# A chunked RWKV layer with a squared-ReLU FFN on one core: state products in four array quarters, a repacked first chunk, and squares on ScalarE

## The chip, the cores and the metric

The kernel runs on one core of one Trainium2 chip. The metric is the time of one execution on the device in microseconds (us); the median of three runs is given. Engines are named as the profile names them: PE is TensorE's matmuls and PEld its weight loads, DVE is VectorE, ACT is ScalarE, POOL is GpSimd, and SP and ACTq are the two queues from which DMAs are issued.

## The reference

For each of 4 batches and 8 heads a state of 48 x 48 runs over 768 tokens; the result, laid out as 3072 tokens x 384, goes through a dense FFN of width 2048 whose activation is the square of a ReLU.

```python
for t in range(S):                                   # S = 768, D = 48
    cur = einsum('bhd,bhe->bhde', u * k[t], v[t])
    y[t] = einsum('bhd,bhde->bhe', r[t], state + cur)
    state = w[t][..., None] * state + einsum('bhd,bhe->bhde', k[t], v[t])
x = y.transpose(0, 2, 1, 3).reshape(B * S, H * D)    # 3072 x 384
h = maximum(x @ w_in, 0.0)                           # 384 x 2048
out = (h * h) @ w_out                                # 2048 x 384
```

## The kernel before

The 768 tokens are cut into six chunks (`c`) of 128. Chunk and batch make a *unit* of attention, 24 in all. The eight heads of a unit lie as four pairs `p`; of a pair, head `j = 0` stands on partitions 0 to 47 and head `j = 1` on partitions 64 to 111, so a pair fills 112 rows. In a unit, w is multiplied up along the tokens by scans (L478), its reciprocal comes from `Ln` and `Exp`, r and k are scaled by both, and then come four kinds of products on PE. `scores` (step `mt`, L526) makes the 128 x 128 score matrices of the heads; DVE puts them under the causal mask into tiles whose diagonal ACT has set (`diag`, L515) from `beta`, the sum over a head of -r k u. `inter` (L552) multiplies the incoming state `Ss[b]` by r and `part` (L560) multiplies values by masked scores; both add into one PSUM bank `yb`, and together they are the step `mix` of the chunks after the first. `outer` (step `dS`, L611) makes the new state. ACT and DVE then split y into two fp32r halves (step `x`, L591 and L592). Chunk 0 has no incoming state.

For chunk 0, r, k and w are loaded with the tokens on the partitions, 192 bytes to a packet, into tiles `st0`; PE transposes them into PSUM (step `turn`, L466). Later chunks are turned by DVE block transposes and DMAs instead. In all chunks `beta` comes from two POOL multiplications (L505, L507) and a DVE sum (L508).

The FFN has 16 slices `f` of width 128. For each, nine products (three rows of 128 inputs, each as three fp32r products) fill a PSUM bank `hp` with 512 tokens, or 256 in half steps (L640); ACT takes the ReLU (L645), DVE squares it (L646), ACT rounds it to fp32r (L648) and DVE takes the rest (L649). Then three products for each batch add to `ob` (L655), which stays in PSUM for the whole chunk. The weights are loaded in eight groups in the first 100 us and split into two fp32r parts by ACT, DVE and POOL in turn (L383 to L404).

All of it is written as steps, each with an engine, a cost, a rank and the tiles that it reads and writes. The class `Plan` plays the steps through with these costs; at each point the step that can start first on its engine goes next, and among equals that of the lower rank. The result is one fixed order of instructions per engine. The ranks are the numbers of the class `Ranks`. Tiles are drawn from pools: there are two PSUM banks `a` for all attention products, two `hp`, and two tiles `q` for split weights and for results on their way out. Where `Plan` sees PE idle in the first 110 us, it inserts *fillers*, transposes of the identity whose result nobody reads (L681). After the plan a flag is made from `far`, which tells whether any w lies outside the range that this way of computing can bear; every engine reads it, and a slow path that follows is skipped.

## Time and profile before

| | us |
|---|---|
| median of 3 runs (lowest, highest) | 550.34 (550.27, 550.54) |
| the profiled execution's own time | 549.26 |
| its span from the first to the last instruction | 547.30 |
| PE busy in the span, fillers among it | 532.6 |
| fillers (L681), 97 in banks `a` and 33 in banks `hp` | 19.5 |
| DVE, ACT, POOL busy | 357.1, 287.3, 102.3 |

The profiled execution is 1.08 us under the median. Its clock for TensorE was granted at 0.996 over the span. Rows of the timeline give the start, the length, the engine, the line of the source, the operation and the number of instructions merged into the row, and in brackets how long the engine had been idle and on whom it had waited. Rows of windows give, for each stretch of time, the busy time of each engine and its instructions. An fp32 matmul of the attention appears in the trace as two instructions (passes); one of the FFN, in fp32r, as one.

### The profile page before, as it was taken

Reading aid. Unit: us, or ns where it says so; the run is one execution under the profiler, and the core shown is the slowest. Engines: PE = TensorE matmul, PEld = TensorE weight load, DVE = VectorE, ACT = ScalarE, POOL = GpSimd, SP = SyncE. Lnnn points to the kernel's source line nnn. Section 1 sums busy time; section 2 is a strip of 40 time slices with the busy share of each in tenths; the row PEclk is TensorE's granted clock in tenths of the full one; section 3 lists DMA queues with packets and bytes.
Section 4 is the critical chain, followed back from the end, with each engine's and each line's share of the span. In section 5 each row is a group of like instructions: output and inputs, shape, how many; then the busy total and the mean of one; then the engine's idle time right before and its main releaser. Section 6 shows DMA issues by size and latency. Waiting matters only on the chain. (4 is left out here: it accounts for less than half of the span.)

```text
span 547.3 us, 10350 instructions
## 1 busy us (share of the span) xinstructions
PE 532.6 (97%) x3930; PEld 474.5 (87%) x3930; DVE 357.1 (65%) x650; ACT 287.3 (52%) x677; POOL 102.3 (19%) x119
## 2 busy tenths in 40 slices
PE   7899999999999999999999999999999999999995
PEld 6778988889998989888888888888888889899994
DVE  5889989999587775958667747656855332333331
ACT  2886885566855845655643654545553332332322
POOL 5335653540212020210302002003000000000000
PEclk9999999999999999999999999999999999999998
DMA  9999699156563825455553723703411000000001
GB/s 164 216 244 272 128 245 206 24 90 136 115 132 64 169 47 105 97 104 99 101 107 62 138 73 60 142 3 73 74 57 30 1 0 16 29 31 1 0 1 62
DMA packets 206456, 50.88 MB, mean 93 GB/s; under 512 B 196161, under 2 KB 201281, under 8 KB 206401
## 3 DMA queue, kind: packets, MB, share of 16 engines
q1 hardware_dynamic: 205680, 49.17, 44.0%
q10 hardware_dynamic: 720, 0.98, 0.6%
q8 instruction: 33, 0.54, 0.4%
q14 instruction: 23, 0.18, 0.1%
HBM read 31.65 MB, written 4.72 MB: 66 GB/s over the span
## 5 line engine op out<-in xcount | busy, mean ns | idle before, releaser
L655 PE MATMUL ob<-wo,g 128*128 128x384 f32 x1152 | 226.9, 341 | 0.5 <-ACT g L648 0.5
L640 PE MATMUL hp<-x,wi 128*128 128x512 f32 (+1 forms) x1062 | 222.7, 355 | 1.4 <-DVE g L649 0.9
L655 PEld LDWEIGHTS ob<-wo,g 128*128 128x128 f32 x1152 | 199.3, 188 | 9.2 <-ACT g L648 0.7
L640 PEld LDWEIGHTS hp<-x,wi 128*128 128x128 f32 x1062 | 174.5, 188 | 27.5 <-DVE g L649 2.3
L645 ACT ACTIVATE t<-hp 128x512 f32<-128x512 f32 (+1 forms) x118 | 61.1, 518 | 154.2 <-PE hp L640 132.5
L646 DVE SCALAR_TENSOR_TENSOR hp<-hp,t 128x512 f32<-128x512 f32 (+1 forms) x118 | 70.3, 596 | 102.0 <-ACT t L645 101.5
L649 DVE TENSOR_TENSOR g<-hp,g 128x512 fp32r<-128x512 f32 (+1 forms) x118 | 68.9, 585 | 38.1 <-ACT g L648 37.3
L648 ACT CAST g<-hp 128x512 fp32r<-128x512 f32 (+1 forms) x118 | 59.5, 505 | 55.7 <-DVE hp L646 55.6
L515 ACT ACTIVATE m<-ident,beta 128x128 f32<-128x128 f32 x192 | 60.4, 395 | 1.2 <-DVE beta L508 1.2
L505 POOL TENSOR_TENSOR st<-st 128x384 f32<-128x384 f32 x24 | 26.6, 1108 | 61.7 <-DVE st L432 54.5
L620 POOL TENSOR_TENSOR S<-S,Ec 112x192 f32<-112x192 f32 x16 | 8.3, 523 | 142.2 <-DVE S L619 142.2
L530 DVE COPY_PREDICATED m<-caus,a 128x512 f32<-128x512 uint8 x48 | 33.3, 730 | 0.7 <-PE a L526 0.6
L478 DVE TENSOR_TENSOR_SCAN pt<-pt,zero 112x128 f32<-112x128 f32 x80 | 30.3, 426 | 3.0 <-DMA v<-in_v_dram 1.3
L526 PEld LDWEIGHTS a<-pt 48*128 48x128 f32 x384 | 23.6, 187 | 7.3 <-issue 5.1
L526 PE MATMUL a<-pt 48*128 48x128 f32 x384 | 28.3, 285 | 1.1 <-DVE pt L498 1.1
L560 PE MATMUL a<-m,v 128*48 128x128 f32 (+1 forms) x384 | 27.2, 279 | 1.0 <-DVE m L530 1.0
L432 DVE STREAM_TRANSPOSE st<-st 128x1152 f32<-128x1152 f32 x20 | 27.2, 1366 | 0.0
L560 PEld LDWEIGHTS a<-m,v 128*48 128x48 f32 (+1 forms) x384 | 20.0, 128 | 6.4 <-issue 4.6
L592 DVE SCALAR_TENSOR_TENSOR x<-a,x 112x128 fp32r<-112x128 f32 (+2 forms) x44 | 17.5, 431 | 12.3 <-ACT x L591 11.7
L507 POOL TENSOR_TENSOR st<-st,un 128x384 f32<-128x384 f32 x24 | 25.1, 1047 | 1.6
L404 POOL TENSOR_TENSOR wi<-q,wi 128x768 fp32r<-128x768 f32 x8 | 17.6, 2204 | 38.0 <-ACT wi L403 31.5
L495 DVE TENSOR_TENSOR pt<-pt,m 112x512 f32<-112x512 f32 x24 | 17.4, 728 | 8.9 <-ACT m L486 8.3
(78 smaller groups left out, 417.1 us busy)
## 6 DMA issues: line engine op xcount, KB each, us to landing
pt<-st SPq DMA_DIRECT2D x80, 96.0 KB, 2.3
ro<-in_moe_w_out_dram SPq DMA_DIRECT2D x8, 768.0 KB, 7.5
v<-in_v_dram SPq DMA_DIRECT2D x24, 192.0 KB, 3.4
st<-in_w_dram SPq DMA_DIRECT2D x11, 384.0 KB, 4.2
st<-in_k_dram SPq DMA_DIRECT2D x11, 384.0 KB, 5.4
st<-in_r_dram SPq DMA_DIRECT2D x11, 384.0 KB, 5.6
pt<-st SPq DMA_DIRECT2D x80, 48.0 KB, 2.5
out_dram<-q SPq DMA_DIRECT2D x20, 192.0 KB, 1.9
```

The costliest lines, as they stand in the source:

```text
L432: V.transpose(out=zt[:, i].rearrange("a t p q i -> a t (p q) i"), in_=sv[:, :, i].rearrange("s t p q x -> s t (p q) x"))
L478: lambda p=p: V.tensor_tensor_scan(out=pt[:, 0, p], data0=src(0)[:, p], data1=zero.broadcast_to([HP, C]), initial=1.0, op0=ALU.mult, op1=A ...
L515: A.activation(mv(j)[:, p], ident, AF.Copy, scale=beta.tile[:, 2 * p + j:2 * p + j + 1])
L526: T.matmul(mts[j].tile.rearrange("s (p t) -> s p t", p=NP)[:, p], pt[js, 2, p], pt[js, 1, p], start=True, stop=True)
L530: lambda j=j: V.copy_predicated(out=mv(j), mask=caus.unsqueeze(1).broadcast_to([128, NP, C]), data=mts[j].tile.rearrange("s (p t) -> s p t ...
L560: T.matmul(ybv()[to:to + n + D, spot(p)], vt.tile[:, o - n:o + D], mv(j)[:, p], start=(c == 0 and p == SPLIT), stop=True, skip_group_check ...
L640: T.matmul(hp.tile[:, 0:n], wi[f][:, wl, kt], xT[:, kt, xl, xs], start=(m == 0), stop=(m == 3 * KT - 1))
L645: P.add("act", 0.5 if full else 0.28, rank("g"), lambda: A.activation(t(), h(), AF.Relu), r=[hp], w=[(g, 1)])
L646: P.add("dve", 0.61 if full else 0.33, rank("g"), lambda: V.scalar_tensor_tensor(out=h(), in0=h(), scalar=0.0, in1=t(), op0=ALU.max, op1=A ...
L648: P.add("act", 0.53 if full else 0.31, rank("g"), lambda: A.copy(out=hi(), in_=h()), r=[hp], w=[(g, 0)])
L649: P.add("dve", 0.61 if full else 0.33, rank("g"), lambda: V.tensor_tensor(out=lo(), in0=h(), in1=hi().bitcast(F32), op=ALU.subtract), r=[h ...
L655: T.matmul(obs[b][:, 0:DM], g.tile[0][:, gl, o:o + C], wo[f][:, wl], start=(f == 0 and m == 0), stop=(f == NF - 1 and m == 2))
```

## The change

1. *State products in four quarters.* `inter` runs the pairs in the order 0, 3, 2, 1. For pairs 3 and 1 (`ACROSS`) the result of head `j` goes to the other half of the PSUM partitions, and into a second bank `far_yb`, in `inter` and in `part`. So the rows used (0 to 47 or 64 to 111) and the columns used (0 to 63 or 64 to 127) make four combinations. `mix` now needs both banks `a`, and y is split in three parts instead of two (`outs`). One weight load of each group is cut in two so that its rows match the swapped halves.
2. *Chunk 0.* w, k and r of a batch come in one DMA each, whose partitions are head and block of 8 tokens: 128 packets of 1,536 bytes instead of 1,024 of 192. `turn` is now 16 products with columns of the identity per tensor (each two passes) instead of 4 transposes. `beta` is formed after the turn: ACT copies -k, DVE multiplies by r, PE multiplies by `ut`, which holds u as columns, and ACT copies the result. `ut` is made from two small DMAs on ACT's queue into a tile `u8` that DVE clears first, one transpose on PE and two ACT copies. `un`, still used by later chunks, is loaded later from SP's queue.
3. *FFN of chunk 0.* Its 22 steps (12 half, 10 full) are squared by ACT.
4. *The last results* go out through four tiles `m`. Batches 0 and 2 are copied by ACT and stored from ACT's queue, 1 and 3 by DVE and stored from SP's; of batch 3, ACT copies one half.
5. *The flag* is made by steps of the plan, with a 1 x 1 product.
6. `Plan` has a changed rule for who may claim tiles, new constants, and all ranks are new (`Ranks`, of which the diff shows a line).

```diff
-    AT = {'load': -105.75, 'z': 279.5, 'pt': 293.75, ...}
+    AT = {'load': 311.75, 'z': -350, 'pt': -3.75, ...}
-    LANES, RUNS, SLACK, START = 8, 2300, 2.0, 2.4
+    LANES, RUNS, SLACK, START = 8, 2300, 2.0, 1.4
-    IDLE = (110.0, 4.0, 0.3, 0.12)
+    IDLE = (110.0, 2.8, 0.3, 0.12)
...
+    ACROSS = (3, 1)
...
-    nc.scalar.dma_start(out=un, in_=u.rearrange("h d -> (h d)").partition_broadcast(128))
+    u8 = P.pools["m"][1][1][0:H, 0:HP]
+    V.memset(u8, 0.0)
+    for j in range(2):
+        nc.scalar.dma_start(out=u8[:, j * J:j * J + D], in_=u)
+    us = Slot("hp")
+    P.add("pe", 0.1, -300, lambda: T.transpose(out=us.tile[0:HP, 0:H], in_=u8, identity=ident[0:H, 0:H]), w=[us])
...
+            for b0 in (b, b + 1) if c == 0 else ():
+                        nc.sync.dma_start(out=st.tile.rearrange("s (t b x) -> s t b x", t=3, b=2)[:, i, b0 - b, 0:TB * D],
+                                          in_=src[b0, :, ss, :].rearrange("h (a s) d -> h a (s d)", s=TB))
...
-                    for p in range(NP):
-                        T.transpose(out=to[:, p], in_=pairs[:, p], identity=ident)
+                    for y in range(TB):
+                        for j in range(2):
+                            n = (J, D)[j]
+                            T.matmul(to[j * J:j * J + n, :, :, y], rows[:, y * D:y * D + n], pick[:, :, j], start=True, stop=True, ...)
...
+        if c == 0:
+            P.add("act", ..., A.activation(pt[:, 2], src(2), AF.Copy, scale=-1.0), ...)
+            P.add("dve", ..., V.tensor_tensor(out=pt[:, 2], in0=pt[:, 2], in1=src(1), op=ALU.mult), ...)
+            def sums():
+                for p in range(NP):
+                    T.matmul(tl(ps[0])[:, 2 * p:2 * p + 2], pt[:, 2, p], ut[:, p], start=True, stop=True, ...)
...
+        side = lambda p, j: 1 - j if p in ACROSS else j
         def inter():
-            for p in (*TILES, SPLIT):
+            for p in (0, 3, 2, 1):
                 for j in range(2):
-                    T.matmul(ybv()[j * J:j * J + n + D, spot(p)], Ss[b][js, ...], pt[js, 1, p], start=(spot(p) == 0), ...)
+                    T.matmul(spot(p)[to:to + n + D], Ss[b][js, ...], pt[js, 1, p], start=(p in (0, 3)), ...)
...
-        P.add("dve", ..., V.scalar_tensor_tensor(out=h(), in0=h(), scalar=0.0, in1=t(), op0=ALU.max, op1=ALU.mult), ...)
+        if c == 0:
+            P.add("act", ..., A.activation(h(), t(), AF.Square), r=[(g, 1)], w=[hp])
+        else:
+            P.add("dve", ..., V.scalar_tensor_tensor(out=h(), in0=h(), scalar=0.0, in1=t(), op0=ALU.max, op1=ALU.mult), ...)
...
-                os_ = Slot("q")
+                os_ = Slot("m" if end else "q")
...
+    P.add("pe", 0.2, rank, lambda: T.matmul(fps.tile[0:1, 0:1], flag, one, start=True, stop=True), r=["flag"], w=[fps])
```

The start of PE before (`ident` is the identity, `st_135` holds w, k and r of batches 0 and 1, `ob` and `a` are PSUM banks):

```order
L681 MATMUL a_145<-ident 128x128 x19
L466 MATMUL ob_139<-ident,st_135 128x128 x4
L681 MATMUL a_145<-ident 128x128 x2
L466 MATMUL ob_141<-ident,st_135 128x128 x4
L681 MATMUL a_145<-ident 128x128 x2
L466 MATMUL ob_140<-ident,st_135 128x128 x4
```

The start of PE after, with what each row waits for (`m_157` is the tile `u8`; the DMAs named in its first row are the two loads of u; the second row holds fillers):

```order
L359 MATMUL hp_145<-ident,m_157 112x8 [waits DMAHW3_49,DMAHW5_49,DVE_49,Pool_49]
L750 MATMUL a_147<-ident 128x128 x17
L497 MATMUL ob_141<-ident,st_135 64x64 [waits DMAHW0_49]
L497 MATMUL ob_141<-ident,st_135 48x64
```

The transpose of u has come to the head of PE, ahead of the fillers and the first turn; there are 81 fillers in all instead of 130, and behind the first FFN product there are 2 of them instead of 31.

The state and value products of one unit on PE before (`S_129` is the state, `a_145` the one bank):

```order
L552 MATMUL a_145<-pt_127,S_129 64x128
L552 MATMUL a_145<-pt_127,S_129 48x128
L552 MATMUL a_145<-pt_127,S_129 64x128
L552 MATMUL a_145<-pt_127,S_129 48x128
L552 MATMUL a_145<-pt_127,S_129 64x128
L552 MATMUL a_145<-pt_127,S_129 48x128 x3
L560 MATMUL a_145<-m_158,v_151 64x128
```

The same place after, with two banks `a_148` and `a_147`:

```order
L706 MATMUL ob_141<-wo_75,g_97 128x384 x3
L599 MATMUL a_148<-pt_127,S_130 64x128
L599 MATMUL a_148<-pt_127,S_130 48x128
L599 MATMUL a_147<-pt_127,S_130 48x128
L599 MATMUL a_147<-pt_127,S_130 64x128
L599 MATMUL a_148<-pt_127,S_130 64x128
L599 MATMUL a_148<-pt_127,S_130 48x128
L599 MATMUL a_147<-pt_127,S_130 48x128 x2
L607 MATMUL a_148<-m_162,v_153 64x128
```

Eight matmuls stay eight, two for each of the four combinations. Over the whole program PE goes 157 times from one kind of array use to another (full, row halves, column halves, quarters) instead of 133 times.

At the end of DVE's program, after, the flag's comparison (L749), which waits for PE's last product, stands ahead of the two copies of results:

```order
L700 TENSOR_TENSOR g_97<-hp_145,g_97 128x512 [waits PE_49,Activation_49]
L749 TENSOR_SCALAR flag_i<-a_147 1x1 [waits PE_49]
L714 COPY m_159<-ob_142 128x384
L714 COPY m_160<-ob_144 128x192 [waits Activation_49]
L757 TENSOR_LOAD flag_i [waits DVE_49]
```

On SP, too, the reading of the flag stands ahead of the two stores of these copies. Before, no result was copied by DVE there.

More of the change, by code (lines that the diff above doesn't have):

```diff
@@ L198 @@
-    LAG = 2
+    AT = {'load': 311.75, 'z': -350, 'pt': -3.75, 'rk': -45.75, 'beta': 190.5, 'far': 301, 'v': 372.5, 'scan': -67.25, 'ln': -130.75, 'rt': -69.25, 'kn': -35, 'diag': 45.75, 'mt': -197.75, 'mask': 253.5, 'ktp': -331.25, 'kt': -191.75, 'mix': -146.25, 'x': -182.25, 'x3': -366.5, 'send': -58.75, 'dS': -74, 'S': -10.25}
+    AT0 = {'load': -134, 'turn': -192.5, 'rk': -234, 'beta': -426.75, 'far': 167.25, 'v': -18.75, 'scan': -53, 'ln': -344.75, 'rt': -84.5, 'kn': -137, 'diag': -76.75, 'mt': -424.25, 'mask': -23, 'ktp': 40.5, 'kt': 228.75, 'mix': -2.75, 'x': -429.5, 'x3': -190.5, 'send': -251, 'dS': -102.25, 'S': 256}
@@ new lines @@
+    AT1 = {'load': 67, 'z': 273.25, 'pt': 29, 'rk': 446, 'beta': 16.75, 'far': -195.5, 'v': 267.25, 'scan': 136, 'ln': -57.25, 'rt': 198.5, 'kn': 72.75, 'diag': 386.5, 'mt': -559.25, 'mask': 9.5, 'ktp': -539.5, 'kt': 139, 'mix': -229.25, 'x': 106.25, 'x3': -193.5, 'send': -227.75, 'dS': -127.75, 'S': -232.5}
+    U0 = (-253.75, -214.25, -115, 73.5)
+    C1 = (-20.75, -24.5, 124.5, 44.25)
+    W0 = (-174, -102.5, -39.75, 50.5, 165.75, 85.5, 71.25, 211.75)
+    WL = (-14, -12.25, 110, 5, 3, -5.25, -285, 23.5)
@@ L200, in unit @@
+    OFF = {'hp': 1, 'g': -172, 'ob': 6.25, 'os': -416.25}
+    LAG = -0.5
     def unit(self, c, b, name):
@@ L680, with bad @@
             x += step
+    flag, one, flag_i = (const.tile([128, 1], t, name=n) for n, t in (("flag", F32), ("one", F32), ("flag_i", I32)))
+    G.memset(one, 1.0)
+    fps = Slot("a")
+    rank = RANKS.unit(NC - 1, B - 1, "far") + 1
+    def bad():
+        V.tensor_reduce(out=flag, in_=far, axis=AX.X, op=ALU.max)
+        V.tensor_scalar(out=flag, in0=flag, scalar1=0.0, scalar2=None, op0=ALU.is_gt)
+    P.add("dve", 0.2, rank, bad, r=[("far", c, b) for c in range(NC) for b in range(B)], w=["flag"])
+    P.add("pe", 0.2, rank, lambda: T.matmul(fps.tile[0:1, 0:1], flag, one, start=True, stop=True), r=["flag"], w=[fps])
+    P.add("dve", 0.1, rank, lambda: V.tensor_scalar(out=flag_i[0:1], in0=fps.tile[0:1, 0:1], scalar1=0.0, scalar2=None, op0=ALU.is_gt), r=[fps], w=["flag_i"])
     P.filler = lambda bank: T.transpose(out=bank[:, 0:128], in_=ident, identity=ident)
```

172 lines of the change are left out of this document (98 added, 74 removed).

## The prediction, made before the changed kernel was timed

> **What bounds the kernel.** I read the page first, then the windows by stage, then the timeline of the start, of one unit of attention, and of the end. The page says that PE is busy almost throughout:
>
> ```profile
> PE 532.6 (97%) x3930; PEld 474.5 (87%) x3930; DVE 357.1 (65%) x650; ACT 287.3 (52%) x677; POOL 102.3 (19%) x119
> ```
>
> That share holds fillers, so I took it apart by stage: first up to the first FFN product (34.71), then to the last filler, then the long middle, and what follows PE's last FFN product. The first five rows are all instructions, with PE, PEld, DVE, ACT and POOL in turn, the last two the fillers alone.
>
> ```profile
> 0.00:34.71 34.71, 29.36 (x272) 24.71 (x272) 26.70 (x61) 21.14 (x54) 17.22 (x33) 1.00 1.06 207
> 34.71:80.00 45.29, 43.15 (x357) 38.66 (x358) 41.06 (x73) 36.70 (x87) 22.06 (x13) 1.00 0.91 213
> 80.00:300.00 220.00, 219.39 (x1772) 197.13 (x1771) 171.84 (x321) 129.96 (x325) 51.13 (x58) 1.00 0.54 105
> 300.00:540.55 240.55, 240.55 (x1534) 213.92 (x1532) 117.34 (x196) 98.52 (x212) 11.87 (x16) 1.00 0.20 42
> 540.55:547.30 6.75, 0.12 (x3) 0.03 (x1) 0.16 (x1) 0.96 (x2) 0.00 (x0) 0.65 0.35 118
> ...
> 0.00:34.71 34.71, 15.34 (x99) 12.90 (x99) 1.00 1.06 207
> 34.71:80.00 45.29, 4.20 (x31) 3.58 (x31) 1.00 0.91 213
> ```
>
> From 80 to 540.55 PE idles 0.61 us: there every microsecond of PE work counts in full. Ahead of 34.71 PE does 29.36 - 15.34 = 14.0 us of real work; 20.7 are filler or idle. From there to 80 another 4.20 + 2.14 = 6.3 are. With the 0.61 that makes 27.6 us of empty time, and the tail is 6.75. So three things can move the end: PE's work, the empty time in the first 80 us, and the tail.
>
> What makes the early time empty is DVE, and ahead of it the first turn:
>
> ```profile
> 1.05 1.50 DVE L307 MEMSET st<- 128x768 f32 x2 [1.05 <-PEq L770]
> 1.61 4.32 PE L681 MATMUL a<-ident 128*128 128x128 f32 x19 [1.61 <-POOL ident masks.py:199]
> 2.56 0.59 DVE L343 MEMSET v<- 128x128 f32 x4
> 6.08 0.89 PE L466 MATMUL ob<-ident,st 128*128 128x128 f32 x4
> 7.01 1.37 DVE L478 TENSOR_TENSOR_SCAN pt<-ob,zero 112x128 f32<-112x128 f32 x4 [2.81 <-PE ob L466]
> 12.21 4.31 PE L681 MATMUL a<-ident 128*128 128x128 f32 x38
> ...
> 7.00:34.71 27.71, 23.65 (x46) 1.00 1.15 226
> 34.71:99.00 64.29, 58.05 (x97) 1.00 0.89 203
> ```
>
> The last two rows are DVE alone: from its first scan it works 23.65 of the 27.71 us to the first FFN product, and 58.05 of 64.29 after that. The filler rows also give PE's pace: 128 columns in 4.32 / 19 = 0.227 us at the start, although the windows show a granted clock of 1.00, and 4.31 / 38 = 0.113 later.
>
> **Quarters.** One unit:
>
> ```profile
> 98.89 1.08 PE L552 MATMUL a<-pt,S 48*64 48x128 f32 x16
> 99.91 1.09 PE L560 MATMUL a<-m,v 128*64 128x128 f32 x16
> 103.57 0.67 PE L611 MATMUL a<-v,m 128*64 128x48 f32 x16
> 104.16 2.37 PE L655 MATMUL ob<-wo,g 128*128 128x384 f32 x12
> ```
>
> The 16 passes of `inter` take 99.91 - 98.89 = 1.02 us. At 0.113 a pass singly they would take 1.81, in pairs 8 x 0.113 = 0.90; so two run at once, and 0.12 goes for the change of array use. Four at once need 4 x 0.113 = 0.45: 0.45 less a unit, 20 units, **-9.0 us**. Bounds: 0 if quarters do not overlap further, -9.0 if they do fully. L560 uses all 128 rows for every pass and also gets 16 passes into 1.02 us, so two column halves already share rows; and L611's 16 passes take 104.16 - 103.57 - 0.12 = 0.47, that is 0.029 each with their weight loads, and four of those fit into 0.12. I take the full end.
>
> [...]
>
> **Added PE work.** `turn`: 32 passes of 64 columns with weights as in L611. 0.029 each if the weight loads set the pace (0.94), 0.039 if columns do (1.25); L611 has the same weights, so 1.0, against 4 x 0.113 = 0.45: 12 x 0.55 = +6.6 (5.9 to 9.6). `sums`: 8 passes with 128 columns of weights and 2 that stream, between 8 x 0.029 = 0.23 and a filler's 8 x 0.113 = 0.90; its weight load is a filler's, so four times 0.90, +3.6 (0.9 to 3.6). Changes of array use: 24 more at about 0.11, +2.6. PE's work: -9.0 + 6.6 + 3.6 + 2.6 = **+3.8**.
>
> **What I cost at nothing.** y is split in three parts, one ACT and one DVE instruction more in each of 20 units:
>
> ```profile
> L591 ACT ACTIVATE x<-a 112x128 fp32r<-112x128 f32 x20 | 5.4, 269 | 1.1 <-PE a L560 1.1
> L592 DVE SCALAR_TENSOR_TENSOR x<-a,x 112x128 fp32r<-112x128 f32 x20 | 5.6, 282 | 3.5 <-ACT x L591 3.5
> ```
>
> Both engines have room behind 80 us (129.96 and 171.84 of 220); uncovered, 0.55 a unit would make 11 us. `mix` now waits for both banks `a`, and FFN products are queued behind it on PE; `scores` has always taken both banks, and PE still idled only 0.61 us. The eight extra DMA issues for weights, the later load of `un`, and the loads of batches 2 and 3, which SP now issues ahead of the first weights, are covered by DVE's 27 us of work ahead of the first FFN product; at 207 GB/s the first 2.8 MB take 13.5 us. If that cover went, a weight group would be late by one DMA's landing, about 5 us. POOL only loses work.
>
> **The empty time.** First the new wait. PE's first instruction needs u, which needs DVE's clearing of `u8`. DVE starts at 1.05; two small clearings, `ut`, the four of L343 (0.59) and the rest put `u8` near 2.1. Then ACT issues two DMAs. Prices for issue and landing:
>
> ```profile
> 540.50 0.34 ACTq L662 DMA_DIRECT2D out_dram<-q  x1
> ...
> x<-x SPq DMA_DIRECT2D x60, 32.0 KB, 2.0
> ...
> un<-in_u_dram ACTq DMA_DIRECT2D x1, 192.0 KB, 4.5
> ```
>
> The second is issued near 2.45 and lands between 4.5 and 7.0; being small, I take 4.9. Behind it, in order on PE, stand 17 fillers at the slow pace, 3.9, then the first turn, 1.0: the first scan starts near 9.8 instead of 7.01. Larger packets help here only if the fillers are not in the way, and they are.
>
> From the first scan to the first FFN product DVE now has 52 instructions instead of 46: four products and two masks more, four instructions of a weight split, one block transpose; three reductions and two state updates fewer.
>
> ```profile
> L432 DVE STREAM_TRANSPOSE st<-st 128x1152 f32<-128x1152 f32 x20 | 27.2, 1366 | 0.0
> L498 DVE TENSOR_TENSOR pt<-pt,m 112x512 f32<-112x512 f32 x20 | 13.7, 684 | 0.2
> L530 DVE COPY_PREDICATED m<-caus,a 128x512 f32<-128x512 uint8 x48 | 33.3, 730 | 0.7 <-PE a L526 0.6
> L508 DVE TENSOR_REDUCE beta<-st 128x8 f32<-128x384 f32 x24 | 12.9, 539 | 0.9 <-POOL st L507 0.9
> L396 DVE SCALAR_TENSOR_TENSOR q<-ro,q 128x768 uint32<-128x768 uint32 x8 | 8.7, 1082 | 0.0
> L619 DVE TENSOR_TENSOR S<-a,S 112x192 f32<-112x192 f32 x16 | 5.6, 352 | 4.3 <-PE a L611 4.1
> ```
>
> 4 x 0.68 + 2 x 0.73 + 4 x 0.9 + 1.37 - 3 x 0.54 - 2 x 0.35 = +6.8; durations overlap a little, so +6. That gives 29.7, and 2.6 of waits (4.1 before): the first FFN product at 42.1. PE's own count agrees: real work 14.0 + 7.1 (twelve turns for eleven) + 2.7 (three `sums`) + 1.1 (one more `mt`) = 24.9, plus 4.9, 3.9, 62 fillers at 0.113 = 7.0 and 1.4 of waits. So 17.3 us are empty there. But now three units and two weight groups are ready instead of two and one.
>
> Behind it, DVE loses the 22 squares:
>
> ```profile
> L646 DVE SCALAR_TENSOR_TENSOR hp<-hp,t 128x512 f32<-128x512 f32 x74 | 51.5, 697 | 95.0 <-ACT t L645 94.9
> L646 DVE SCALAR_TENSOR_TENSOR hp<-hp,t 128x256 f32<-128x256 f32 x44 | 18.8, 426 | 7.0 <-ACT t L645 6.6
> ```
>
> 12 x 0.43 + 10 x 0.70 = 12.1 us less where DVE had 6.2 to spare. ACT takes them at about L645's price (0.38 and 0.60): 10.6 more on some 49 of 64 us. So I leave 1.7 of the 6.9 us of later emptiness, 0.2 of it fillers. Empty time: 19.0 against 27.6, **-8.6** (-5 to -12).
>
> **The tail.**
>
> ```profile
> 540.71 0.16 DVE L696 TENSOR_SCALAR flag_i<-a 128x1 int32<-128x1 f32 x1 [3.71 <-PE a L694]
> 541.47 0.48 ACT L660 COPY q<-ob 128x384 f32<-128x384 f32 x1 [1.00 <-DMA out_dram<-q]
> 542.41 0.48 ACT L660 COPY q<-ob 128x384 f32<-128x384 f32 x1 [0.47 <-SPq L698]
> 542.92 1.02 ACTq L662 DMA_DIRECT2D out_dram<-q  x1
> ```
>
> Copies no longer wait for two buffers. But the flag's comparison, which ends at 540.87, now stands ahead of DVE's two copies, and SP reads the flag ahead of its stores: the last store is issued near 542, not 542.92. **-1.0** (0 to -2).
>
> **Sum.** +3.8 - 8.6 - 1.0 = -5.8. The profiled execution took 549.26, which becomes 543.5; the median of the runs lies 1.08 above, so **544.5 us**.
>
> **Rivals.** (a) *Slower:* quarters that share rows do not overlap. The term of 9.0 falls away, and the added turns and sums stay: 553.5. It decides from the point where less than 3.2 of the 9.0 are had. For it speaks that no row shows more than two passes at once; against it L560 and L611. 10%. (b) Half of the overlap, with weight loads of the four in each other's way: 549.0. 9%. (c) u lands early or the fillers do not delay the first turn, and the scan starts at 7 after all: 541.7. Large packets speak for it, the order of PE against. 15%. (d) ACT becomes what DVE was: the squares wait behind `diag` and weight splits, and the 5.2 us that I took out behind the first FFN product come back: 549.7. ACT's 49 + 10.6 of 64 us speak for it. 14%. (e) Writing the turned tensors in steps of 32 bytes doubles a turn; twelve more microseconds, half of them in empty time: 550.5. No row shows such writes. 7%.
>
> **Numbers.** The forecast has 45%. Measurements of this kernel tell a change from none at about 0.2%, 1.1 us: 549.2 to 551.4 is no change. Faster: the forecast, (c), and about two thirds of (b) and (d), 0.78; the same 0.10; slower, (a) and the upper ends of (d) and (e), 0.12. The range 539.5 to 550.5 leaves out (a) and some of (c) and (e).
>
> **What would show it.** Right: a quarter row of 16 passes with some 0.57 us to the next row; the first scan near 9.8; the first FFN product near 42 and hardly a filler after it; the last store near 542. Wrong: 1.0 us for the quarters, PE waiting on ACT's square between 45 and 130 us, or, since both banks `a` go to one `mix`, new idle time of PE before products into `a` behind 130.

## The result, and the profile after

| | us |
|---|---|
| changed kernel, median of 8 runs (lowest, highest) | 547.41 (546.44, 549.32) |
| kernel before, median of 8 runs on the same chip | 550.54 (549.46, 551.28) |
| ratio, 95% interval | 0.9946 (0.9931 to 0.9961) |
| the profiled execution's own time, its span | 547.43, 545.6 |

The change makes the kernel faster by 3.1 us; 5.8 were forecast. The direction was right, and the size is about half. In the pair of profiled executions the span went from 547.3 to 545.6, by 1.7 us only, because the profiled execution of before (549.26) was faster than all eight of its runs here.

The page of the kernel after, its line of busy times:

```profile
PE 530.7 (97%) x4250; PEld 470.7 (86%) x4250; DVE 351.2 (64%) x652; ACT 300.4 (55%) x728; POOL 92.8 (17%) x111
```

The windows of the kernel after by the same stages: to the first FFN product (now 44.85), to 80, to 300, to the end of the last FFN product, and what follows it. The last two rows are its fillers (L750) alone, with PE and PEld.

```profile
0.00:44.85 44.85, 37.67 (x632) 33.63 (x633) 33.98 (x72) 27.13 (x68) 12.09 (x29) 1.00 0.84 217
44.85:80.00 35.15, 35.03 (x288) 32.19 (x287) 28.73 (x50) 31.30 (x77) 16.45 (x10) 1.00 0.89 195
80.00:300.00 220.00, 220.00 (x1866) 194.74 (x1865) 175.28 (x340) 146.19 (x379) 53.26 (x61) 1.00 0.65 115
300.00:537.83 237.83, 237.83 (x1470) 210.17 (x1468) 112.24 (x191) 95.44 (x205) 11.02 (x13) 1.00 0.18 35
537.83:545.60 7.77, 0.12 (x3) 0.02 (x2) 0.97 (x3) 0.32 (x1) 0.00 (x0) 0.65 0.31 104
...
0.00:44.85 44.85, 12.14 (x79) 10.21 (x79) 1.00 0.84 217
44.85:80.00 35.15, 0.38 (x2) 0.24 (x2) 1.00 0.89 195
```

Read as the prediction read them: PE's real work is 530.65 - 12.52 = 518.1 us (before 532.56 - 19.54 = 513.0), so +5.1. Ahead of the first FFN product 44.85 - 37.67 + 12.14 = 19.3 us are idle or filler, behind it 0.12 + 0.38 = 0.5: 19.8 against 27.6, so -7.8. The tail is 7.77 against 6.75, so +1.0. The sum is -1.7, which is the difference of the spans.

The start, from the timeline of the kernel after, PE first, then DVE:

```profile
5.72 0.23 PE L359 MATMUL hp<-ident,m 8*112 8x8 f32 x1 [5.72 <-DMA m<-in_u_dram]
5.88 3.89 PE L750 MATMUL a<-ident 128*128 128x128 f32 x17
9.70 4.54 PE L497 MATMUL ob<-ident,st 128*64 128x64 f32 x128
15.15 2.08 PE L497 MATMUL hp<-ident,st 128*64 128x64 f32 x64
...
44.85 2.40 PE L688 MATMUL hp<-x,wi 128*128 128x256 f32 x18
...
11.49 1.37 DVE L509 TENSOR_TENSOR_SCAN pt<-ob,zero 112x128 f32<-112x128 f32 x4 [8.60 <-PE ob L497]
...
11.49:44.85 33.36, 31.99 (x55) 1.00 0.97 244
```

The last row is a window with DVE alone: from its first scan to the first FFN product DVE works 31.99 of 33.36 us. By this row the lead of the FFN hangs on the first scan, and that on u and the slow fillers, as forecast, only 1.7 us later than forecast. But the chain of work that ended last by 46 us, as the profile follows it back, goes another way: over SP's issues and the landings of loads, among them two of weights (`ri`) and one of a later `k`. Its longest pieces, with start and length:

```profile
13.83 7.91 DMA ri<-in_moe_w_in_dram
21.75 7.18 DMA ri<-in_moe_w_in_dram
28.95 6.56 DMA st<-in_k_dram
```

So two readings of the start stand side by side, and the experiments have to decide.

One unit after, from PE's timeline: the state products L599 now take 103.56 - 102.96 = 0.60 us to the next product, where L552 took 1.02. Over all 20 units, from the start of the sixteen passes to the next product, it is 11.95 us against 20.28.

```profile
102.96 0.67 PE L599 MATMUL a<-pt,S 48*64 48x128 f32 x16
103.56 1.09 PE L607 MATMUL a<-m,v 128*64 128x128 f32 x16
```

And the tail: flag, copies and SP's two stores.

```profile
537.76 0.19 PE L748 MATMUL a<-one,flag 128*1 128x1 f32 x2
537.86 0.37 ACTq L720 DMA_DIRECT2D out_dram<-m  x1
537.99 0.15 DVE L749 TENSOR_SCALAR flag_i<-a 1x1 int32<-1x1 f32 x1 [3.71 <-PE a L748]
538.06 0.92 DVE L714 COPY m<-ob 128x384 f32<-128x384 f32 x2
538.27 0.32 ACT L718 COPY m<-ob 128x192 f32<-128x192 f32 x1 [0.45 <-PE a L748]
539.10 0.81 SPq L720 DMA_DIRECT2D out_dram<-m  x2
```

SP's last store is issued at 539.53, 1.70 us behind the last FFN product (537.83); before, the last one was issued 2.37 behind it. So the issue did come earlier. But of the last store's 16 parts, 13 landed by 541.47 and three at 542.09, 542.86 and 543.67, 5.84 us behind the last product; before, the last part landed at 545.57, 5.02 behind it. Late parts are not new: before, three parts of the last store but one landed 1.2 us behind its other 13.

### The profile page after: what moved, and what is told of

Same layout as the page of the kernel before. It is cut to its first block, busy times and chain, and to the rows that moved or that the text cites. A ratio compares the mean times of both kernels' runs of the same rounds, so it can differ in the third digit from the quotient of the medians.

```text
span 545.6 us, 11056 instructions
## 1 busy us (share of the span) xinstructions
PE 530.7 (97%) x4250; PEld 470.7 (86%) x4250; DVE 351.2 (64%) x652; ACT 300.4 (55%) x728; POOL 92.8 (17%) x111
## 4 chain that ended last, share of the span: by engine, by line
PE 90%; DMA 5%; SPq 1%; DVE 1%; ACT 1%; issue 0%; DVEq 0%
PE hp L688 38%; PE ob L706 38%; PE a L607 4%; PE a L567 4%; DMA ri<-in_moe_w_in_dram 3%; PE a L599 2%; PE a L659 2%; PE a L579 1%; DMA st<-in_k_dram 1%; SPq L444 1%; DMA st<-in_r_dram 1%; ACT m L556 0%; SPq L391 0%; PE a L621 0%; DVE m L571 0%
## 5 line engine op out<-in xcount | busy, mean ns | idle before, releaser
L697 DVE SCALAR_TENSOR_TENSOR hp<-hp,t 128x512 f32<-128x512 f32 (+1 forms) x96 | 58.1, 606 | 90.9 <-ACT t L693 90.7
L640 DVE SCALAR_TENSOR_TENSOR x<-a,x 112x128 fp32r<-112x128 f32 (+2 forms) x64 | 20.6, 344 | 24.6 <-ACT x L639 23.0
L639 ACT ACTIVATE x<-a 112x128 fp32r<-112x128 f32 (+2 forms) x64 | 18.5, 323 | 21.0 <-PE a L607 16.6
L607 PE MATMUL a<-m,v 128*48 128x128 f32 (+1 forms) x384 | 26.9, 279 | 0.4 <-DVE m L571 0.2
L538 POOL TENSOR_TENSOR st<-st 128x384 f32<-128x384 f32 x20 | 20.9, 1050 | 37.4 <-DVE st L459 37.4
L607 PEld LDWEIGHTS a<-m,v 128*48 128x48 f32 (+1 forms) x384 | 19.8, 128 | 5.7 <-issue 4.2
L525 POOL COPY Ec<-pt 112x4 f32<-112x4 f32 x20 | 6.0, 300 | 103.8 <-DVE pt L509 103.8
L540 POOL TENSOR_TENSOR st<-st,un 128x384 f32<-128x384 f32 x20 | 21.3, 1071 | 1.3
```

The costliest lines, as they stand in the source:

```text
L607: T.matmul(spot(p)[to:to + n + D], vt.tile[:, o - n:o + D], mv(j)[:, p], start=(c == 0 and p == SPLIT), stop=True, skip_group_check=True)
L697: P.add("dve", 0.61 if full else 0.33, rank("g"), lambda: V.scalar_tensor_tensor(out=h(), in0=h(), scalar=0.0, in1=t(), op0=ALU.max, op1=A ...
```

## The experiments

The first theory was: the quarters pay in full because four passes in four quarters stand next to each other; the rest of the change pays less than forecast because the start is late (u and the fillers) and the flag stands in the tail. The rival for the start: not PE's start, but the loads of weights, issued by SP behind twelve loads of chunk 0, hold the first FFN product. Fifteen kernels were run, each timed in five rounds beside the kernel before. That kernel's medians in these groups were 550.60, 550.51, 551.11 and 550.73, so times of different groups can be compared to about half a microsecond.

### The order of the passes

```diff
-            for p in (0, 3, 2, 1):
+            for p in (0, 2, 3, 1):
```

> The changed kernel with the state products' pairs of heads in the order 0, 2, 3, 1 instead of 0, 3, 2, 1: the same 16 passes a unit, but the two that stand next to each other use the same two quarters as the two ahead of them. If four quarters run at once only when they stand next to each other, a unit goes back from 0.60 to about 1.0 us, 20 units make +8.3, and the time is near 555.7 (the changed kernel's median is 547.41). If the saving came from something else (two banks, the longer list of passes), a unit stays near 0.60 and the time at 547.4.

547.44 us. The line group of L599 has 13.6 us of busy time against 13.4, and the units make 12.22 us against 11.95. My theory of neighbours fell: here the order does not matter. In the trace the first pass of pair 3 starts 0.03 us after the first of pair 0, although pair 2 stands between them in the list. So in this run passes of another quarter go past those that wait for their own; in the changed kernel passes of one quarter start 0.11 to 0.15 us apart, and four of different quarters within 0.03.

### Two quarters instead of four

```diff
-        side = lambda p, j: 1 - j if p in ACROSS else j
+        side = lambda p, j: j
```

> The changed kernel with heads j of all pairs in column half j, so that the state products use two quarters of the array (as before the change) and not four; the two banks, the order of the pairs and all else stay. Heads of two pairs end in each other's rows of y, so this leaves out that the result is the reference's. If the number of quarters makes the 0.42 us a unit, a unit takes 1.0 again and the time is near 555.7. If it is the two banks or the list's order, a unit stays at 0.60 and the time at 547.4.

556.52 us, 9.1 more than the changed kernel. Its timeline has the old unit again:

```profile
104.35 1.08 PE L599 MATMUL a<-pt,S 48*64 48x128 f32 x16
105.36 1.09 PE L607 MATMUL a<-m,v 128*64 128x128 f32 x16
```

1.01 us, and 20.29 over the 20 units, with the same two banks and the same list. The number of quarters is the cause. By the rows it is worth 8.3 us, by the medians 9.1; in this run's profiled execution the granted clock also fell, to 0.85 between 16 and 22 us, and its two executions with the highest mean clock, 0.997 and 0.998, took 555.63 and 555.31, 8.2 and 7.9 more than the changed kernel. So the saving arrives in the time, since PE is the limit where these units stand: in the changed kernel it idles 0.12 us between 44.85 and 537.83.

### Squares by DVE again

```diff
-            P.add("act", ..., lambda: A.activation(h(), t(), AF.Square), ...)
+            P.add("act", ..., lambda: V.scalar_tensor_tensor(out=h(), in0=h(), scalar=0.0, in1=t(), op0=ALU.max, op1=ALU.mult), ...)
```

> The changed kernel with DVE again making the squares of chunk 0's FFN steps, at the places of the lists where ACT's stood. Theory one, DVE is still short behind the first FFN product: 12.1 us more work for it in 45 to 130 us, some 4 to 5 us of PE idle or filler come back, 552. Theory two, with three units and two weight groups ready at the first FFN product DVE has room for them: within 1 us of 547.4.

556.52 us: 9.1 more again, so theory one, and by the median at twice its price. (The lists of work stay those that were made for squares on ACT.) The waits of PE behind the first FFN product, and three windows of that run:

```profile
PE a L567 <- DVE pt L546: 3.3, 2, 2.2
...
45.39:80.00 34.61, 33.58 (x278) 30.40 (x277) 30.41 (x58) 25.31 (x62) 14.98 (x9) 1.00 0.90 194
80.00:130.00 50.00, 48.08 (x343) 39.96 (x342) 48.00 (x73) 37.71 (x82) 19.25 (x16) 1.00 0.62 133
130.00:180.00 50.00, 47.83 (x445) 44.12 (x447) 40.97 (x81) 27.72 (x80) 12.44 (x14) 0.97 0.60 101
```

PE idles 1.03 + 1.92 + 2.17 = 5.1 us where the changed kernel idles 0.12, DVE is at 48.00 of 50 from 80 to 130, and the first FFN product comes 0.5 us later. The rest shows as slower products; the granted clock of 0.97 from 130 to 180 makes 1.5 us of it by my estimate (0.03 of 50). The six executions tell more: one, at a mean clock of 0.999, took 553.11 us, 5.7 more than the changed kernel, and five at 0.991 and 0.992 took 555.39 to 558.72. So some 5.7 us, about PE's idle time and the later start, are what the squares are worth at a steady clock (one execution), and the remaining 3.4 go with a lower clock, whose cause is not shown.

### u behind the first turns

In the order of work, the two steps of u are moved behind the third turn, and the first turn gets 12 fillers instead of 17.

```diff
+        turns = [s for s in out if s.fn.__name__ == "turn"][:3]
+        first = [s for s in out if s.rank == -300]
+        out = [s for s in out if s.rank != -300]
+        i = out.index(turns[2]) + 1
+        out[i:i] = first
+        turns[0].fill = 12, turns[0].fill[1]
```

> The changed kernel with the transpose of u and the two copies behind it moved behind the first three turns, and 12 instead of 17 fillers ahead of the first turn; all else stands in the same order. Theory one, the start holds: the first turn no longer waits for u (5.61) and for 3.9 us of cold fillers behind it, but for its load, which lands at 4.43 in the changed kernel: first turn near 4.5, first scan near 6.3 instead of 11.49. DVE is busy for 32 of the 33.4 us from there to the first FFN product, so that product comes 3 to 5 us earlier than 44.85 and the time falls to about 543.5. Theory two, the loads hold: the first weight group's landing (DVE's work on it starts at 25.2, part of it lands at 28.9) comes no earlier, the gained time is lost in waits of DVE for loads, the first FFN product stays within 1 us of 44.85 and the time within 1 us of 547.4.

548.39 us (ratio 0.9956, 0.9941 to 0.9972): nothing gained. Its timeline by engine and one window:

```profile
6.49 1.36 DVE L517 TENSOR_TENSOR_SCAN pt<-ob,zero 112x128 f32<-112x128 f32 x4 [3.60 <-PE ob L505]
...
23.39 0.91 ACT L412 ACTIVATE q<-ri 128x768 f32<-128x768 f32 x1 [2.10 <-DMA ri<-in_moe_w_in_dram]
...
24.34 0.56 DVE L416 TENSOR_SCALAR q<-q 128x768 uint32<-128x768 uint32 x1 [1.73 <-ACT q L412]
...
44.92 2.38 PE L696 MATMUL hp<-x,wi 128*128 128x256 f32 x18
...
16.00:30.00 14.00, 11.84 (x192) 11.33 (x193) 10.24 (x18) 9.74 (x27) 0.65 (x2) 0.76 1.01 233
```

The scan is 5.0 us earlier, exactly as theory one wanted, and the first FFN product stays at 44.92. At 23.4 ACT has waited 2.10 us for the first weights, and DVE behind it. Theory two, then, for this kernel; but the clock of 0.76 between 16 and 30 took a part too. Of the eleven executions two, at a mean clock of 0.995 and 0.994, took 546.18 and 546.24 us, and nine at 0.986 to 0.992 took 547.96 to 550.84. Where the clock holds, u late gains about 1.2 us, still far from the 3.9 of theory one.

### Sixteen landings a load

The loads of chunk 0 are quoted from the view of DMAs of the first 22 us, before and after:

```profile
DMA packets 12628, 4.01 MB, mean 182 GB/s; under 512 B 11859, under 2 KB 11987, under 8 KB 12627
```

```profile
DMA packets 4271, 3.72 MB, mean 169 GB/s; under 512 B 2303, under 2 KB 3839, under 8 KB 4269
```

A third of the packets, and no more bytes a second. The six loads of batches 0 and 1 finished at 5.94, 6.82, 8.02, 9.22, 10.42 and 11.67 before and at 4.43, 5.97, 7.25, 8.21, 9.57 and 10.55 after; the trace shows 16 landings for each load of before and 9 for each of after. The DMA's outer dimension after is the 8 heads; of the 9 landings eight come with the data (3.98 to 4.43 for the first load) and one some 0.4 us behind the end of the issue (at 2.00). The prediction read the larger packets and not this. That the eight go with the 8 heads was a guess, so I put the 16 blocks of tokens outside:

```diff
-    in_=src[b0, :, ss, :].rearrange("h (a s) d -> h a (s d)", s=TB))
+    in_=src[b0, :, ss, :].rearrange("h (a s) d -> a h (s d)", s=TB))
...
-    pick = ident.rearrange("s (p j x) -> s p j x", p=NP, j=2)
+    pick = ident.rearrange("s (x p j) -> s p j x", p=NP, j=2)
```

> The changed kernel with the loads of w, k, r of chunk 0 written with the 16 blocks of tokens as the outer dimension and the 8 heads inside (the rows then lie in another order, and the turns pick other columns of the identity). In the changed kernel each such load left 9 landings, where a load of before left 16. If the outer dimension of 8 spread each load over 8 of the 16 DMA engines, 16 landings appear and the loads follow each other at about 0.65 us (SP's issue) instead of 1.25. Theory one (the start hangs on u, the fillers and then DVE): the first turn stays at 9.7 and the time within 0.7 us of 547.4. Theory two (the loads hold the first FFN product): it comes 2 to 3 us earlier, and the time is near 545.

555.17 us (ratio 1.0086): neither theory. The loads did what was hoped: 16 landings each, the six done at 3.95, 4.62, 5.37, 6.21, 6.88 and 8.17, and SP issues the first weight group at 10.01 instead of 11.87, its second part at 13.58 instead of 19.82. But the edit had a price of its own. The same two turns of the timeline:

```profile
18.22 3.97 PE L497 MATMUL hp<-ident,st 128*64 128x64 f32 x64
```

64 passes in 3.97 us where the kernel after takes 2.08: the moving side now reads the identity in steps of 8 columns, 32 bytes. The prediction's rival (e) priced such a doubling for strided writes; here it comes with strided reads.

```diff
+    perm = const.tile([128, 128], F32, name="perm")
+    G.tensor_copy(out=perm.rearrange("s (h a) -> s h a", h=8), in_=ident.rearrange("s (a h) -> s h a", h=8))
...
-    pick = ident.rearrange("s (x p j) -> s p j x", p=NP, j=2)
+    pick = perm.rearrange("s (p j x) -> s p j x", p=NP, j=2)
```

> As the run with 16 blocks of tokens as outer dimension (16 landings a load, the first weight group issued from 10.0 instead of 11.9, its second half at 13.6 instead of 19.8), but the turns pick from a copy of the identity whose columns lie in the turns' order, so that the moving side is read in runs of 16 again. If the doubled turn there (32 passes in 1.98 us instead of 0.93) came from the stride of that read, a turn is back near 0.95. Theory one, u and the cold fillers and then DVE hold the first FFN product: first turn at 9.5, DVE's 33 us behind it, 44.5 and a time near 547. Theory two, the loads of weights hold it: it comes 2 to 3 us earlier, near 42, and the time is near 545.

547.53 us (0.9947). The turn is back (64 passes in 2.08 us), and the time is that of the changed kernel: theory one for this edit. Its profiled execution was the slowest of its runs (550.37, with the clock at 0.83 from 20 to 30), so its first FFN product at 46.88 is not typical.

> The same loads and turns, and u's transpose behind the first three turns with 12 fillers ahead of the first. If two chains of nearly the same length end at the first FFN product (u, fillers, DVE; and the queue of loads to the first weight group, on which ACT waited 2.1 us when u alone was moved), then taking both shorter brings what neither brings alone: first scan near 6.3, first FFN product at 40 to 41.5 instead of 44.85, time 543.5 to 545. If PE's granted clock, which fell to 0.83 to 0.87 between 6.5 and 30 when u alone was moved, is what takes the gain back, the product stays above 43.5 and the time above 546.5.

544.46 us (0.9883, 0.9868 to 0.9899). The timeline of that run:

```profile
4.36 4.47 PE L507 MATMUL ob<-perm,st 128*64 128x64 f32 x96
...
41.51 2.40 PE L698 MATMUL hp<-x,wi 128*128 128x256 f32 x18
...
9.97 0.69 DVE L539 TENSOR_TENSOR pt<-pt,ob 112x512 f32<-112x512 f32 x1 [2.23 <-ACT pt L538]
```

Either edit alone gives nothing in the median, both together 3.0 us: the first FFN product has two chains of nearly the same length behind it, u and the fillers with DVE's 33 us on one side, SP's queue of twelve loads ahead of the first weights on the other. I had named the second in the prediction and costed it at nothing, covered by the first. A fallen clock alone does not explain the 3 us: in the profiled execution of a later run with both edits and an early flag it fell to 0.76 between 16 and 22, and the first FFN product still came at 41.55.

```profile
16.00:22.00 6.00, 6.00 (x109) 0.76 1.08 266
```

### The packets and turns undone

Loads and turns of before in the places of the new ones, the lists otherwise unchanged, without and with u late:

```diff
-    in_=src[b0, :, ss, :].rearrange("h (a s) d -> h a (s d)", s=TB))
+    in_=src[b0, :, ss, :].rearrange("h s d -> s h d"))
...
-    T.matmul(to[j * J:j * J + n, :, :, y], rows[:, y * D:y * D + n], pick[:, :, j], ...)
+    T.transpose(out=to[:, p], in_=pairs[:, p], identity=ident)
```

> The changed kernel, its lists of work unchanged, with the old loads (192 bytes a packet) and the old turns (four transposes of 128 columns) in the places of the packed loads and the turns by products; the sums on PE, u, the squares, the quarters and the flag stay. The larger clearing of the pads delays DVE's clearing for u by about 1 us. Theory one, the packed loads as made bring no earlier data (they landed at 1.25 us apiece over half of the landings, as the old ones did at 1.2) and cost 6.7 us of PE's time: some of that is on the way to the first FFN product, and the time falls by 0 to 3 us to 544.5 to 547.4. Theory two, SP's queue fills with 1,024 packets a load, twelve loads stand ahead of the weights, the first weight group is issued several us later than at 11.9, and the time rises by 3 or more.

> The same with u behind the first three turns and 12 fillers, so that the first turn waits for its load alone. Against the run with 16 landings a load and u behind (544.46) this tells what packed loads bring at their best. Theory one: nothing, the turns' extra PE time eats it: 544 to 546. Theory two: the loads of weights are late behind twelve small-packet loads, as in the run with 8 heads outside (548.39): 548 or more.

548.85 us (0.9971, 0.9958 to 0.9984) and 548.59 (0.9959, 0.9944 to 0.9974). Between the two theories: SP issues the first weight group at 15.60 instead of 11.87, but its second part already at 19.14, before the 19.82 of the changed kernel. The first scan moves from 11.49 to 12.87, as the longer clearing of pads delays u (ACT copies it at 8.37 instead of 5.99); that is as much as the 1.4 us of the median, but the clock was lower too, 0.78 and 0.74 between 16 and 30, so the two are not separated. With u late, ACT waits for the first weights as in the run with packed loads and u late, a little longer:

```profile
24.12 0.90 ACT L412 ACTIVATE q<-ri 128x768 f32<-128x768 f32 x1 [2.82 <-DMA ri<-in_moe_w_in_dram]
```

So with u late the packed loads as they were made bring next to nothing (548.59 against 548.39), and with 16 landings 4.1 us (548.59 against 544.46). In the profiled execution with old packets and u late, PE's clock fell more than in any other (PE alone):

```profile
16.00:22.00 6.00, 6.00 (x29) 0.50 1.25 206
```

All twelve executions of that run have a mean clock of 0.979 to 0.985, so this one is typical. How much of the 4.1 us is that clock and how much the loads is open.

### The kernel before with parts of the change

Quarters alone, in the kernel before with its own ranks; then with the squares on ACT as well:

```diff
+    ACROSS = (3, 1)
...
-            for p in (*TILES, SPLIT):
+            for p in (0, 3, 2, 1):
```

> The kernel before with the four quarters alone: state products in two banks and four quarters, y in three parts, the weight rows to match; loads, turns and the bonus term of chunk 0, the squares on DVE, the flag and the last results as before, ranks and planner's constants as before. Theory one: the quarters are worth here what they are worth in the changed kernel (9.1, from the run with two quarters): 541.5. Then all the rest of the change together costs 6 us, although its squares on ACT save 9. Theory two: the quarters pay less without the rest, because PE's saved time goes into waits for DVE or for the second bank: 545 or more.

> The same with the squares of chunk 0's FFN steps on ACT as well, so the change without the packed loads, the turns by products, the sums on PE, the flag's place and the four last buffers. Theory one: DVE is the limit behind the first FFN product there too, where the kernel before had 6.3 us of filler and idle up to 80 us: 4 to 5 us less than quarters alone, near 537, and the packed loads with what they bring are the part that loses. Theory two: in this order the weights' loads are the limit behind the first FFN product, and the squares change nothing: 541.5.

555.17 and 559.77 us: both slower than the kernel before. For the quarters that is theory two in kind, but far beyond its number; for the squares neither held. The units' passes make 11.95 us in both, so the quarters work; what they save goes into waits and fillers. PE's idle and filler time is 34.3 us before, 41.4 with the quarters and 48.4 with the squares as well. Fillers of the quarters alone, with PE and PEld:

```profile
34.80:60.00 25.20, 1.24 (x9) 0.77 (x7) 0.86 1.04 243
60.00:80.00 20.00, 4.63 (x39) 4.40 (x40) 1.00 0.72 175
```

and with the squares:

```profile
34.80:60.00 25.20, 3.87 (x31) 3.31 (x29) 1.00 1.06 243
60.00:80.00 20.00, 12.23 (x107) 11.75 (x107) 1.00 0.78 188
```

The kernel before has 2.57 and 1.63 there. The first run also gets a clock of 0.86 between 34.8 and 60, and its six executions have mean clocks of 0.987 to 0.991, where the kernel before has 0.996. The tails of the two, with the end of the kernel before, are 7.85 and 7.68 us, where that kernel's own profiled execution has 6.75. With other tile claims and costs the old ranks give another order, and these two runs test that order as much as the quarters. What the new start as a whole is worth against the old one, each with an order made for it, therefore stays open; a search for new ranks was not tried.

### The tail

```diff
-    rank = RANKS.unit(NC - 1, B - 1, "far") + 1
+    rank = -1000
```

> The changed kernel with the flag's reduction, product and comparison as soon as the last term is there (near 370 us) instead of behind the last FFN products. Theory one, the flag stands in the way of the last copies and stores: both DVE copies start at 537.7 instead of 538.06, the last store is issued half a microsecond earlier, the flag is read long before, and the tail behind the last FFN product goes from 7.75 to 6.5 or 7: 546.2 to 546.7. Theory two, the tail is set by instruction fetches behind the skipped branch, which hold parts of the last store: the tail stays at 7.5 to 8 and the time at 547.4.

547.76 us (0.9942, 0.9926 to 0.9957): not to be told from the changed kernel by the time. In the trace the tail is 6.64 instead of 7.77, and one part of the last store still lands at 544.61, 2.09 behind the other fifteen. So the first theory has the size of the tail, and the second the part that is left. In the profiled execution PE's weight loads also stood still for 1.48 us up to 69.43, behind a DVE that had waited 1.86 us for a transfer.

```diff
-    any_bad = nc.values_load(flag_i[0:1, 0:1], min_val=0, max_val=1)
-    with tc.If(any_bad > 0):
+    if False:
```

> The changed kernel without the reading of the flag and without the branch and the slow path behind it (so inputs with large decay would not be handled; the flag is still computed). If instruction fetches at the skipped branch (24 to 32 KB near 540) hold parts of the last two stores, which landed at 542.09 to 543.67 where their other parts landed by 541.47, then all parts land by 541.5 and the tail goes from 7.78 to about 5.5: 545.2. If the fetches are hidden behind the stores' own landing, the tail stays above 7 and the time at 547.

546.49 us (0.9918, 0.9899 to 0.9937). The windows of this run:

```profile
45.23:540.25 495.02, 492.82 (x3620) 437.05 (x3618) 316.26 (x578) 273.23 (x660) 80.76 (x84) 1.00 0.43 81
540.25:545.34 5.09, 0.12 (x3) 0.02 (x2) 0.97 (x3) 0.32 (x1) 0.00 (x0) 0.96 0.40 148
```

The tail is 5.09, and all parts of the last store land within 3.67 us of the last product. Against the changed kernel's profiled execution the branch and SP's reading of the flag together cost 2.7 us of the tail, and 1.6 to 2.7 against the ten profiled executions with flag and branch as changed, whose tails are 6.69 to 7.77. Up to half a microsecond of that is the issue, since SP no longer reads the flag ahead of its stores (0.80 instead of 1.27 behind the last product). That the rest is the fetch of instructions (five packets, 0.05 MB, behind 537.8 in the changed kernel) was argued from the fetches' times, not isolated, and the late parts are no fixed price of the branch: with the branch and an early flag one execution below has none. By the time the two kernels are not told apart, since the intervals of the ratios overlap. The first row shows what else this execution lost: PE idled 2.2 us in the middle, where a DVE scan at 176 waited 2.39 us for a transfer (pt). Such a stall of DVE for that transfer, 0.7 to 2.4 us near 170 to 177, is in six of the fifteen profiled executions and not in the one of the changed kernel; it may well make part of the spread of its runs.

### Together

> The changed kernel with 16 landings a load, u behind the first three turns, and the flag computed near 370 us: the three together. The first two gave 544.46. If the last store's landing follows its issue, as in the run with the early flag (tail 6.64 instead of 7.78), 1.1 less: 543.4. If the landing hangs on instruction fetches, 544.4.

543.25 us (0.9865, 0.9849 to 0.9881), as expected; the tail of its profiled execution is 4.74, and no part of the last store lands late. In the next one u stands behind the first turn instead of the third:

```diff
-            i = out.index(turns[2]) + 1
+            i = out.index(turns[0]) + 1
```

> The run that was the fastest (16 landings a load, u late, early flag: 543.25), with u's transpose behind the first turn instead of the third. In the run with 16 landings and u late DVE stood still for 2.23 us at 7.7 to 9.97, because ACT's copy of u (waiting for the transpose behind the third turn) stands ahead of its copy of k. u lands at 5.6, the first turn ends near 6.2: the copy comes about 2 us earlier, DVE's work and the first FFN product 1 to 2 us: 541.5 to 542.5. If the loads of weights end last, nothing: 543.2.

542.43 us (0.9854, 0.9837 to 0.9872). The timeline:

```profile
9.16 0.69 DVE L539 TENSOR_TENSOR pt<-pt,ob 112x512 f32<-112x512 f32 x1 [1.42 <-PE ob L507]
...
40.44 2.38 PE L698 MATMUL hp<-x,wi 128*128 128x256 f32 x18
```

DVE's wait is 1.42 us and now for PE's turns, where it was 1.60 for ACT in the run above and 2.23 in the one with the late flag; the first FFN product comes at 40.44 instead of 41.55. This is the lowest median: 5.0 us under the changed kernel, 8.3 under the one before. Its 0.8 us against the run above are not clear of the noise: four executions each, and their times overlap.

## Why the prediction was half right

*Quarters, -9.0: right, 0.7 too much.* -8.3 by the rows, 9.1 by the medians of the run with two quarters. The reading of L560 and L611 (passes that share rows overlap when their columns differ: 16 of L560 in 1.02 us to the next row, 16 of L611 in 0.59) was right. Two quarters share each group of rows, and the passes overlapped all the same: they started four at a time, 16 of them in 0.60 us.

*PE's work, +3.8 in all: 1.3 short.* Half of that is the quarters' 0.7. The turns made +6.7 (forecast +6.6; the upper price of 0.039 for a pass stands on no row, and a pass took 0.0325), the sums 3.9 (3.6). What is left of the measured +5.1 is 2.8 us, against the 2.6 put down for changes of array use, whose price was an estimate from the 0.12 left over in one unit and which no run isolates; `part` (L607) has 1.25 of it, 25.12 us instead of 23.87 over all units. Rival (e), a turn doubled by strided writes, did not come: 64 passes took 2.08 us.

*Empty time, -8.6: nearly right, -7.8, though its steps were off.* u came at 5.72, not 4.9; the 17 fillers ended as forecast 3.9 later; the first turn then took 1.8 and not 1.0 to the scan, since its passes still ran at PE's slow pace (two every 0.107 us to 10.9, every 0.056 from 11.1). The scan was at 11.49 instead of 9.8, the first FFN product at 44.85 instead of 42.1, with 33.4 instead of 32.3 of DVE between. Most of that was made good because almost nothing was empty behind it: 0.5 instead of 1.7. The squares on ACT are the reason. I took 5.2 out for them; the run with DVE's squares shows 9.1 by the medians and 5.7 in its execution with the highest clock. Rival (d), ACT in DVE's place, did not come.

*The cover of the loads: wrong.* "Covered by DVE's 27 us" was true only by a hair. With u late, ACT waited 2.10 us for exactly those loads, and DVE 1.73 behind it. Rival (c) priced an early scan at -2.8; the scan at 6.49 gave nothing in the median and 1.2 in the executions at the higher clock.

*The tail, -1.0: the step that failed most, +1.0.* The earlier issue was right, by 0.67 us. That an earlier store ends earlier was not: parts of the last two stores land up to 2.3 us behind the rest, and in the run without branch and reading of the flag they do not. In the pair of profiled executions that step missed by 2.0 of the 4.1 us between the forecast of the span's change (-5.8) and what the spans show (-1.7). In other executions it missed by about 1: tails with the new end are 6.69 to 7.77, with the old end 6.75, 7.68 and 7.85. So no gain is the firm part, and a longer tail is not shown; what holds the late parts back stays open.

*The median.* The kernel before had a median of 550.54 in the 8 runs, 1.28 above its profiled execution, while the changed kernel's profiled execution lay at its median. So 1.3 of the 4.1 us are not in the medians, and the time missed by 2.9: 547.41 against 544.5. That is chance and no merit of the forecast, which had carried an offset of 1.08 from before to after; the short tail of 6.75 may be a part of it.

*The chances.* The forecast, (c) and two thirds of (b) and (d) add up to 0.75, not to the 0.78 given for faster.

## What to carry over

When one edit takes a stall away and the time does not move, look for a second chain that ends at the same point, and shorten both before giving either up: here each gave nothing in the median and both gave 3 us. Here SP issued twelve early loads ahead of the first weights (11.87), so "covered" should come with the margin by which it is covered. And count the landings of a DMA beside its packets: with 1,536 bytes to a packet in both runs, six loads ended 1.22 us apart with 9 landings each and 0.84 apart with 16.

## What was not expected of the hardware

- Products in different quarters of the array passed each other: with eight passes of two quarters listed ahead of eight of the other two, 16 passes took 0.61 us, where they took 0.60 alternating.
- A DMA of 128 packets of 1,536 bytes with 8 as its outer dimension left 9 landings, and six in a row ended 1.22 us apart on average; with 16 outside it left 16, and they ended 0.84 apart.
- A moving operand read in steps of 32 bytes made the passes of a turn take 62 ns each instead of 32.
- PE's products ran at a slow pace, 0.21 us for 128 columns, for 3.2 to 6 us from the first one (from 5.72 to 10.9 in the changed kernel, from 1.60 to 6.1 and to 7.5 in two runs with u late, from 5.83 to 9.0 in the one without the branch), over fillers and turns alike, and with a granted clock of 1.00 in the windows.
- Between 8 and 60 us the granted clock fell below 0.97, down to 0.50, in nine of the fifteen profiled executions, also where PE had been busy (0.85 from 16 to 22 in the run with two quarters, behind 8.00 busy us of 8); what sets it off is not settled.
